# Cosine attention and GELU feed-forward on one core: swapped row sums added by tensor_reduce, values at piece ends, a first batch in a new order

## The chip, the core and the metric

The kernel runs on one core of a Trainium2 chip. TensorE (PE) multiplies matrices, VectorE (DVE), ScalarE (ACT) and GpSimd (POOL) work on rows of up to 128 partitions, and SyncE (SP) issues most of the transfers. Each engine takes its instructions in the order in which they stand in the program and waits for the others by semaphores. The metric is device time in microseconds (us), median of several runs.

## The reference

```python
q_n = q / (norm(q, axis=-1, keepdims=True) + 1e-06)          # q, k, v: (8, 12, 448, 64) float32
k_n = k / (norm(k, axis=-1, keepdims=True) + 1e-06)
scores = matmul(q_n, k_n.transpose(0, 1, 3, 2)) / tau        # tau = 0.1
attn = exp(scores - max(scores, axis=-1, keepdims=True))
attn = attn / (sum(attn, axis=-1, keepdims=True) + 1e-09)
x = matmul(attn, v).transpose(0, 2, 1, 3).reshape(8 * 448, 768)
h = x @ w_in                                                 # (768, 2048)
out = (0.5 * h * (1 + erf(h / sqrt(2)))) @ w_out             # (2048, 768); out is (3584, 768) float32
```

## The kernel before

The work goes batch by batch, and each batch of 12 heads goes in three groups of four heads (`g` counts the groups: `NQ = 3` a batch, 24 in all). A group passes these stations:

- `load_qk` brings q and k into a tile `qk` (four buffers, issued by SP). `square` squares them into `sq`, and `reduce` (DVE) adds the squares of each row into `nq`. `root` takes the square root as Ln and Exp on ACT (`lq`, `sr`), adds 1e-6 (`se`) and takes the reciprocal on DVE (`rn`). `scale` multiplies q and k by it into bf16 (`qkb`). From unit 3 on, squares and scales are POOL's. The list `units` cuts group 0 into two halves, so that unit numbers run one ahead of group numbers; `groups` says which units share one pass of `root`.
- `transposes` turns `qkb` into `qkT`: for the first batch on PE through PSUM with a copy by DVE, later by a transposing DMA on SP's queue.
- `scores` makes 7 passes a group: 4 matmuls into `st` and one exponential on ACT into `pt`. No maximum is subtracted, since the scores of unit vectors are bounded by 1/tau.
- `sums` multiplies by ones into the bank `sm`, where the row sums of a pair of heads stand in four stripes of 32 partitions, each sum as two halves in neighbouring stripes. `reciprocals` (DVE) transposes the bank (`tr`), swaps neighbouring stripes with four copies of 32 partitions x 28 numbers (`sw`), adds (`su`), takes reciprocals (`rc`) and spreads them by two transposes (`rs`). `values` multiplies `pt` by v into two PSUM banks (`o`), and `normalise` (DVE) multiplies these by `rs` into `x`. `both` is sums, reciprocals, values, normalise in this order.

Then `first(b)` computes `hp = x @ w_in` in 16 column tiles of 6 matmuls each and GELU on ACT. Its first 16 matmuls need only the first two groups of heads, the rest needs `x` of the third. The second product (`op`) of an earlier batch is cut into single matmuls, 16 to a *piece* (`second_pieces`), which `attention(b, fill)` strews between the passes: `plan` says how many of the 96 or 128 run ahead of each step `i`, and each step makes two passes (`group(b, i)`). Steps 5, 8 and 11 have `both`.

Pieces, `hp` tiles, PE transposes and the second bank of `values` take turns in two PSUM banks (`mm_tile`): with `aside=0` the values take the bank that the next piece wants, with `aside=1` the bank of the piece before, which a DVE copy (`ot`) empties. The first batch has no second product to strew; its order is written out in `attention_first`, with a few idle matmuls (`spin`). All orders are by hand; nothing reschedules them.

Of the kernel before, what the change touches and what calls it, by code (L numbers as in the profile page):

```python
# [8 lines left out]
F32 = mybir.dt.float32  # L9
# [6 lines left out]
def kernel(  # L16
# [81 lines left out]

    units = [(0, 0, 1), (0, 1, 2)] + [(g, 0, 2) for g in range(1, NG)]
    NU = len(units)  # L100
    groups = [[n] for n in range(NQ + 1)]
    for n in range(NQ + 1, NU, NQ):
        groups += [[n, n + 1], [n + 2]]
    place = {u: (n, j) for n, gr in enumerate(groups) for j, u in enumerate(gr)}
    qk_t, v_t, sq_t, nq_t, rn_t, qkb_t, qkT_t, pt_t = {}, {}, {}, {}, {}, {}, {}, {}
# [24 lines left out]
        for j in range(m):  # L130
            v_t[g + j] = t[:, j]

    def square(u):
        g, s0, s1 = units[u]
        if s0 == 0:
            sq_t[g] = sqp.tile([128, 2, 2, C, D], F32, tag="sq", name=f"sq{g}")
        sq, t = sq_t[g][:, :, s0:s1], qk_t[g][:, :, s0:s1]
        if u == 0:
            nc.scalar.activation(sq[:, 1], t[:, 1], AF.Square)
            nc.vector.tensor_tensor(sq[:, 0], t[:, 0], t[:, 0], ALU.mult)  # L140
        elif u == 1:
            nc.scalar.activation(sq, t, AF.Square)
        elif u == 2:
            nc.vector.tensor_tensor(sq[:, 0], t[:, 0], t[:, 0], ALU.mult)
            nc.gpsimd.tensor_tensor(sq[:, 1], t[:, 1], t[:, 1], ALU.mult)
        else:
            nc.gpsimd.tensor_tensor(sq, t, t, ALU.mult)  # L147

    def reduce(u):
# [41 lines left out]
    def transposes(u):  # L191
        g, s0, s1 = units[u]
        qkb = qkb_t[g]
        if s0 == 0:
# [7 lines left out]
        for i in range(2):  # L202
# [135 lines left out]

    def attention_first():
        x_t[0] = xp.tile([128, KD, S], BF16, tag="x", name="x0")  # L340
        scores(0, ((0, 0), (0, 1)))
        upto(root, 2)
        upto(scale, 2)
        upto(load_wi, 1)
        scores(0, ((0, 2), (0, 3)))
        upto(reduce, 3)
        upto(transposes, 2)
        scores(0, ((0, 4), (0, 5)))
        upto(root, 3)
        upto(square, 4)  # L350
        scores(0, ((1, 0), (1, 1)))
        upto(scale, 3)
        upto(reduce, 4)
        upto(load_v, 2)
        scores(0, ((1, 2), (1, 3)))
        upto(transposes, 3)
        upto(root, 4)
        scores(0, ((1, 4), (1, 5)))
        upto(scale, 4)
        upto(load_wi, 2)  # L360
        scores(0, ((0, 6), (1, 6)))
        spin(2)
        for c in range(C):
            if c == 2:
                sums(0)
                reciprocals(0)
            if c == 4:
                upto(transposes, 4)
            if c == 5:
                values(0)  # L370
                normalise(0)
            scores(1, ((0, c), (1, c)))
            if c == 0:
                upto(load_qk, 4)
            if c == 1:
                upto(load_wi, 3)
                upto(square, 5)
            if c == 3:
                upto(reduce, 5)
            if c == 4:  # L380
                upto(load_wi, 4)
        for c in range(C):
            if c == 2:
# [102 lines left out]
    upto(square, 1)  # L486
    upto(reduce, 1)
    upto(root, 1)
    upto(square, 2)
    upto(scale, 1)  # L490
    upto(transposes, 1)
    upto(reduce, 2)
    upto(square, 3)
    spin(2)
# [50 lines left out]
```

## Time and profile before

| | |
|---|---|
| median of 3 runs (lowest, highest) | 537.62 us (535.86, 537.73) |
| profiled execution, its own time | 534.5 us |
| its span, first to last instruction | 532.7 us |
| PE, DVE, ACT, POOL busy | 439.4, 243.7, 242.9, 171.5 us |
| mean granted clock of TensorE | 0.923 of full speed |

A busy share is an average over stages with different limits, so it does not say what an edit is worth; the stage in which the edit stands does. A granted clock of 1.00 is 2.4 GHz, 0.50 is 1.2 GHz.

### The profile page before, as it was taken

The numbers are of one execution on the slowest core, as the hardware profiler recorded it, in microseconds if no ns is written. First come the engines' busy times: TensorE is split into PE (matmuls) and PEld (weight loads), VectorE is DVE, ScalarE is ACT, GpSimd is POOL, SyncE is SP. The second block draws the span as 40 slices with busy tenths as digits, with TensorE's granted clock in tenths as the row PEclk, the third lists the DMA queues.
The fourth block names the chain that finished last, engine by engine and source line by source line (L and its number), as shares of the span: only waits on it lengthen the run. The fifth ranks groups of instructions, "written<-read, shape, count | busy, mean of one in ns | idle before, by whom it ended". The sixth has DMA issues, their size and how long they took to land.

```text
span 532.7 us, 8122 instructions
## 1 busy us (share of the span) xinstructions
PE 439.4 (82%) x3428; PEld 211.9 (40%) x3428; DVE 243.7 (46%) x387; ACT 242.9 (46%) x351; POOL 171.5 (32%) x113
## 2 busy tenths in 40 slices
PE   6626996859979599685997959777897959989996
PEld 3203442324435244242543425333353524434553
DVE  6596426582066801578026750557306591054011
ACT  4525465514655048341475326642365604762500
POOL 4871627070342505224061520807016070200000
PEclk9568999888999899797999989979799998999999
DMA  8896997172083902618037360635406440032013
GB/s 289 212 186 105 205 205 155 32 158 109 1 148 97 237 0 43 146 42 225 1 64 152 90 177 0 106 84 119 146 2 116 126 103 0 1 65 61 1 30 90
DMA packets 68340, 54.99 MB, mean 103 GB/s; under 512 B 40400, under 2 KB 63312, under 8 KB 68304
## 3 DMA queue, kind: packets, MB, share of 16 engines
q1 hardware_dynamic: 55888, 42.35, 31.2%
q0 software_dynamic: 12112, 11.80, 14.4%
q8 instruction: 27, 0.44, 0.4%
q10 hardware_dynamic: 304, 0.33, 0.2%
q14 instruction: 9, 0.07, 0.0%
HBM read 45.61 MB, written 11.01 MB: 106 GB/s over the span
## 4 chain that ended last, share of the span: by engine, by line
issue 44%; PE 23%; POOL 21%; DVE 8%; DMA 2%; ACT 1%; SPq 0%; POOLq 0%; DVEq 0%
PE hp L451 10%; POOL sq L147 10%; POOL qkb L187 9%; PE op L287 8%; DVE sw L253 4%; PE st L216 2%; PE o L241 1%; PE sm L230 1%; DMA qk<-in_k_dram 1%; ACT pt L220 1%; DVE rs L260 1%; POOL v L127 1%; DVE nq L157 1%; DVE x L266 1%; DVE tr L249 1%
## 5 line engine op out<-in xcount | busy, mean ns | idle before, releaser
L220 ACT ACTIVATE pt<-st 128x896 bf16<-128x896 f32 x168 | 145.2, 914 | 102.8 <-PE st L216 102.3
L451 PE MATMUL hp<-x,wi 128*128 128x448 bf16 x768 | 161.6, 373 | 34.1 <-DVE x L266 34.1
L287 PE MATMUL op<-wo,g 128*128 128x384 bf16 x896 | 162.8, 333 | 31.1 <-DVE x L266 31.1
L472 ACT ACTIVATE g<-hp 128x448 bf16<-128x448 f32 x128 | 67.6, 543 | 155.2 <-PE hp L451 155.1
L287 PEld LDWEIGHTS <-g 128*128 128x128 bf16 x896 | 83.5, 99 | 105.5 <-issue 57.4
L451 PEld LDWEIGHTS <-wi 128*128 128x128 bf16 x768 | 77.5, 102 | 117.5 <-issue 56.0
L174 POOL TENSOR_SCALAR se<-sr 128x56 f32<-128x56 f32 (+1 forms) x14 | 4.4, 312 | 266.4 <-ACT sr L173 266.4
L187 POOL TENSOR_TENSOR qkb<-qk,rn 128x896 bf16<-128x896 f32 (+1 forms) x48 | 79.1, 1674 | 13.8 <-DVE rn L176 13.8
L253 DVE COPY sw<-tr 32x28 f32<-32x28 f32 x96 | 72.3, 753 | 1.8
L176 DVE RECIPROCAL rn<-se 128x28 f32<-128x28 f32 (+2 forms) x18 | 6.9, 385 | 139.6 <-POOL se L174 139.4
L147 POOL TENSOR_TENSOR sq<-qk 128x1792 f32<-128x1792 f32 x22 | 69.9, 3178 | 0.2
L298 DVE COPY ot<-op 128x384 f32<-128x384 f32 x55 | 29.6, 539 | 70.7 <-PE op L287 70.7
L216 PE MATMUL st<-qkT 64*64 64x448 bf16 x672 | 56.8, 386 | 3.2 <-ACT pt L220 2.8
L157 DVE TENSOR_REDUCE nq<-sq 128x28 f32<-128x1792 f32 (+2 forms) x26 | 48.3, 1861 | 23.6 <-POOL sq L147 23.5
L241 PE MATMUL o<-pt,v 64*64 64x448 bf16 x672 | 38.4, 361 | 12.7 <-DVE qkT L206 12.1
L216 PEld LDWEIGHTS <-qkT 64*64 64x64 bf16 x672 | 17.5, 109 | 35.9 <-issue 30.5
L249 DVE STREAM_TRANSPOSE tr<-sm 128x448 f32<-128x448 f32 x24 | 15.5, 647 | 35.0 <-PE sm L230 35.0
L241 PEld LDWEIGHTS <-v 64*64 64x64 bf16 x672 | 18.8, 109 | 30.2 <-issue 21.4
L260 DVE STREAM_TRANSPOSE rs<-rc 128x448 f32<-128x448 f32 x48 | 28.1, 624 | 0.8
L266 DVE TENSOR_TENSOR x<-o,rs 128x448 bf16<-128x448 f32 x48 | 26.9, 597 | 2.4 <-PE o L241 2.4
L230 PE MATMUL sm<-pt,ones 128*32 128x448 bf16 x336 | 23.9, 371 | 0.4 <-ACT pt L220 0.4
L230 PEld LDWEIGHTS <-ones 128*32 128x32 bf16 x336 | 8.2, 98 | 13.0 <-issue 9.5
(38 smaller groups left out, 93.5 us busy)
## 6 DMA issues: line engine op xcount, KB each, us to landing
out_dram<-ot SPq DMA_DIRECT2D x54, 192.0 KB, 2.7
qk<-in_q_dram SPq DMA_DIRECT2D x23, 448.0 KB, 5.2
qk<-in_k_dram SPq DMA_DIRECT2D x23, 448.0 KB, 5.9
v<-in_v_dram POOLq DMA_DIRECT2D x7, 672.0 KB, 8.5
wi<-in_moe_w_in_dram POOLq DMA_DIRECT2D x8, 384.0 KB, 7.7
wo<-in_moe_w_out_dram POOLq DMA_DIRECT2D x4, 768.0 KB, 11.7
qk<-in_q_dram SPq DMA_DIRECT2D x2, 224.0 KB, 3.5
v<-in_v_dram POOLq DMA_DIRECT2D x1, 448.0 KB, 8.3
```

Of the source, the lines that this page charges most:

```text
L147: nc.gpsimd.tensor_tensor(sq, t, t, ALU.mult)
L157: nc.vector.tensor_reduce(nq[:, part], sq[:, part], mybir.AxisListType.X, ALU.add)
L187: eng.tensor_tensor(qkb[:, i, :, s0:s1].rearrange("p c s d -> p s c d"), t[:, i, s0:s1], rn[:, i].to_broadcast([128, s1 - s0, C, D]), ALU. ...
L216: nc.tensor.matmul(st[cols, n, :S], lhsT=qkT[rows, 1, c, cols], rhs=qkT[rows, 0, :, cols], start=True, stop=True, tile_position=(64 * s, 6 ...
L220: nc.scalar.activation(pt[:, :m], st[:, :m, :S], AF.Exp, scale=inv_tau)
L230: nc.tensor.matmul(bank_t[g, "sm"][r:r + 32, :S], lhsT=ones, rhs=pt_t[g, s, c], start=(c < 2), stop=(c >= C - 2), tile_position=(0, r))
L241: nc.tensor.matmul(bank_t[g, h][cols, :S], lhsT=v_t[g][rows, s, c, :], rhs=pt_t[g, s, c][rows], start=(c == 0), stop=(c == C - 1), tile_po ...
L253: nc.vector.tensor_copy(sw[32 * j:32 * (j + 1)], sums2[32 * (j ^ 1):32 * ((j ^ 1) + 1)])
L260: nc.vector.transpose(rs, rc[:, h].to_broadcast([128, NB, 32]))
L287: nc.tensor.matmul(ps[:, :NH], lhsT=g_t[sb][:, kf, t * 128:(t + 1) * 128], rhs=wo[:, kf, ni * NH:(ni + 1) * NH], start=(kf == 0), stop=(kf ...
L451: nc.tensor.matmul(hps[m], lhsT=wi[:, kd, m * 128:(m + 1) * 128], rhs=x_t[b][:, kd, :], start=(kd == 0), stop=(kd == KD - 1))
L472: nc.scalar.activation(g_t[sb][:, m, hf * S:(hf + 1) * S], hps.pop(m), AF.Gelu)
```

## The change

Five edits, in this order in the diff.

1. In `reciprocals` the four copies into `sw` become four `tensor_reduce` instructions that sum one number each, from the neighbouring stripe into column 1 of `tr` itself; the addition becomes a `tensor_reduce` over columns 0 and 1.
2. `plan` gives other numbers of fill matmuls, so that `both` in steps 5, 8 and 11 comes when a whole number of pieces has been issued. By the unchanged rule in its call, `aside` is then 1 at all three.
3. The `reduce` of step 4 moves to step 6, behind the first `both`.
4. The first batch is written in another order, `attention_first` now holding also what stood ahead of it; squares and scales of units 0 to 3 are split over ACT, DVE and POOL.
5. Units 5 and 6 (groups 4 and 5) share one `root`, and so `first(0)` scales and transposes group 3 alone; group 4 follows in step 1 of `attention(1)`.

```diff
-    groups = [[n] for n in range(NQ + 1)]
-    for n in range(NQ + 1, NU, NQ):
+    groups = [[n] for n in range(NQ + 2)] + [[NQ + 2, NQ + 3]]
+    for n in range(2 * NQ + 1, NU, NQ):
         groups += [[n, n + 1], [n + 2]]
...
-        for i, eng in enumerate((nc.vector if u <= 1 else nc.gpsimd, nc.gpsimd)):
+        for eng, i in parts or ((nc.gpsimd, 0), (nc.gpsimd, 1)):
...
-        sums2 = tr.rearrange("p b (k r) -> p k b r", k=2)[:, :, :, 0]
-        sw = rcp.tile([128, 2, NB], F32, tag="sw", name=f"sw{g}")
+        tr4 = tr.rearrange("p b (k r) -> p k b r", k=2)
         for j in range(4):
-            nc.vector.tensor_copy(sw[32 * j:32 * (j + 1)], sums2[32 * (j ^ 1):32 * ((j ^ 1) + 1)])
+            o = j ^ 1
+            nc.vector.tensor_reduce(tr4[32 * j:32 * (j + 1), :, :, 1], tr4[32 * o:32 * (o + 1), :, :, 0:1],
+                                    mybir.AxisListType.X, ALU.add)
         su = rcp.tile([128, 2, NB], F32, tag="su", name=f"su{g}")
-        nc.vector.tensor_tensor(su, sums2, sw, ALU.add)
+        nc.vector.tensor_reduce(su, tr4[:, :, :, 0:2], mybir.AxisListType.X, ALU.add)
...
     def attention_first():
+        square(2, ((AC, Q),))
+        scale(1, ((DV, 0), (GP, 1)))
+        square(3, ((GP, Q),))
+        scale(2, ((DV, 0), (GP, 1)))
...
+                scale(3, ((DV, 0), (GP, 1)))
                 sums(0)
...
-        plan = {96: (0, 18, 8, 8, 8, 0, 8, 8, 0, 8, 8, 22),
-                128: (0, 22, 12, 12, 12, 0, 12, 12, 0, 12, 12, 22)}[len(fill)]
+        plan = {96: (0, 18, 10, 10, 10, 0, 8, 8, 0, 8, 8, 16),
+                128: (0, 22, 14, 14, 14, 0, 16, 16, 0, 8, 8, 16)}[len(fill)]
...
             if i == 1:
-                upto(scale, nu)
-                upto(transposes, nu)
+                for n in (nu - 1, nu):
+                    upto(scale, n)
+                    upto(transposes, n)
...
-            if i in (4, 9):
-                upto(reduce, nu + (1 if i == 4 else 2))
+            if i in (6, 9):
+                upto(reduce, nu + (1 if i == 6 else 2))
...
-        for n in (nu + 1, nu + 2):
+        for n in (nu + 1, nu + 2) if b else (nu + 1,):
             upto(scale, n)
             upto(transposes, n)
```

Where the instructions stand, at three places. First, DVE in batch 1 (the second batch) at the first `both`; before:

```order
L298 COPY ot_1_869<-op_1_0_868 128x384
L157 TENSOR_REDUCE nq_964<-sq_913 128x28
L249 STREAM_TRANSPOSE tr_981<-sm_966 128x448
L253 COPY sw_983<-tr_981 32x28 x4
L255 TENSOR_TENSOR su_988<-tr_981,sw_983 128x28
```

and of the change:

```order
L295 COPY ot_2_922<-op_2_0_921 128x384
L243 STREAM_TRANSPOSE tr_988<-sm_973 128x448
L249 TENSOR_REDUCE tr_988<-tr_988 32x2x14 x4
L252 TENSOR_REDUCE su_994<-tr_988 128x28
L254 RECIPROCAL rc_996<-su_994 128x28
L257 STREAM_TRANSPOSE rs_0_998<-rc_996 128x448
L257 STREAM_TRANSPOSE rs_1_1000<-rc_996 128x448
L263 TENSOR_TENSOR x_842<-o_0_1002,rs_0_998 128x448
L263 TENSOR_TENSOR x_842<-o_1_1003,rs_1_1000 128x448
L151 TENSOR_REDUCE nq_1073<-sq_914 128x28
```

The sum of the norms' squares (`nq`) stood ahead of the transpose of the row sums and now stands behind `x`; one more piece is copied out (`ot`) ahead of it.

Second, POOL from `first(0)` into batch 1, where `sq_713` and `qkb_872` (before), `sq_706` and `qkb_871` (changed) are group 5; before:

```order
L187 TENSOR_TENSOR qkb_697<-qk_347,rn_674 128x2x7x64 x2
L187 TENSOR_TENSOR qkb_702<-qk_488,rn_674 128x2x7x64 x2
L147 TENSOR_TENSOR sq_713<-qk_491 128x1792
L174 TENSOR_SCALAR se_842<-sr_843 128x28
L187 TENSOR_TENSOR qkb_872<-qk_491,rn_846 128x2x7x64 x2
```

and of the change:

```order
L181 TENSOR_TENSOR qkb_698<-qk_336,rn_675 128x2x7x64 x2
L142 TENSOR_TENSOR sq_706<-qk_497 128x1792
L168 TENSOR_SCALAR se_836<-sr_837 128x56
L181 TENSOR_TENSOR qkb_866<-qk_390,rn_840 128x2x7x64 x2
L181 TENSOR_TENSOR qkb_871<-qk_497,rn_840 128x2x7x64 x2
```

The scaling of group 4 (`qkb_702` before, `qkb_866` now) has moved behind `se`, which waits for ACT in batch 1.

Third, DVE in the first batch from the norms of group 2 (`qk_133`) to the row sums of group 0 (`sm_361`, `sm_364`); before:

```order
L170 TENSOR_REDUCE se_313<-root_1_119 128x28
L176 RECIPROCAL rn_316<-se_313 128x28
L249 STREAM_TRANSPOSE tr_376<-sm_361 128x448
L253 COPY sw_378<-tr_376 32x28 x4
L255 TENSOR_TENSOR su_383<-tr_376,sw_378 128x28
```

and of the change:

```order
L164 TENSOR_REDUCE se_356<-root_1_119 128x28
L170 RECIPROCAL rn_359<-se_356 128x28
L181 TENSOR_TENSOR qkb_361<-qk_133,rn_359 128x2x7x64
L200 COPY qkT_407<-tp_0_408 128x896
L200 COPY qkT_407<-tp_1_417 128x896
L243 STREAM_TRANSPOSE tr_426<-sm_364 128x448
L249 TENSOR_REDUCE tr_426<-tr_426 32x2x14 x4
```

DVE now scales the q of group 2 itself, and its two copies of that group's transposes have moved from behind the row sums of group 0 to ahead of them.

## Rows read from the trace of the kernel before

**Rows 1.** Stretches: start:end, length, busy us per engine, PEclk, DMA share, GB/s.

```profile
0.00:55.70 55.70, 32.19 (x295) 14.71 (x295) 38.21 (x61) 24.44 (x35) 32.50 (x33) 0.75 0.90 198
55.70:74.05 18.35, 18.35 (x99) 9.30 (x96) 5.58 (x9) 7.82 (x15) 10.18 (x6) 1.00 1.32 189
74.05:111.32 37.27, 30.72 (x307) 14.30 (x307) 18.31 (x34) 22.07 (x28) 14.45 (x10) 0.95 0.47 120
111.32:489.05 377.73, 319.03 (x2512) 151.80 (x2509) 174.54 (x271) 179.88 (x256) 114.42 (x67) 0.93 0.39 90
```

**Rows 2.** Stretches as in rows 1: one 128-fill attention, one `hp`, the last attention.

```profile
137.17:173.97 36.80, 33.95 (x340) 16.69 (x339) 19.44 (x36) 22.19 (x28) 14.39 (x9) 1.00 0.42 92
429.61:456.76 27.15, 21.46 (x100) 10.01 (x96) 11.15 (x11) 7.93 (x15) 6.49 (x4) 0.87 0.22 45
456.76:489.05 32.29, 29.34 (x307) 14.01 (x307) 12.79 (x34) 21.59 (x26) 3.61 (x3) 1.00 0.19 43
```

**Rows 3.** Who waited for whom: us in total, times, longest us.

```profile
PE hp L451 <- DVE x L266: 34.1, 6, 5.7
PE op L287 <- DVE x L266: 31.1, 11, 5.1
```

**Rows 4.** Groups of instructions by shape: count, busy us, mean ns of one.

```profile
L253 DVE COPY sw<-tr 32x28 f32<-32x28 f32 x96 | 72.3, 753 | 1.8
L187 POOL TENSOR_TENSOR qkb<-qk,rn 128x448 bf16<-128x448 f32 x2 | 2.7, 1370 | 2.2 <-DVE rn L176 2.2
L170 DVE TENSOR_REDUCE se<-root 128x28 f32<-128x56 f32 x2 | 0.4, 206 | 0.5 <-ACT root L169 0.5
```

**Rows 5.** Timeline (start us, us, instruction, [idle before]) around batch 2's third row sums.

```profile
170.69 6.63 POOL L187 TENSOR_TENSOR qkb<-qk,rn 128x896 bf16<-128x896 f32 x4 [0.62 <-DVE rn L176]
173.31 7.18 DVE L253 COPY sw<-tr 32x28 f32<-32x28 f32 x4
177.28 3.17 POOL L147 TENSOR_TENSOR sq<-qk 128x1792 f32<-128x1792 f32 x1
182.86 18.16 PE L451 MATMUL hp<-x,wi 128*128 128x448 bf16 x80 [5.69 <-DVE x L266]
```

**Rows 6.** Timeline around the first row sums of batch 1.

```profile
85.51 2.02 DVE L157 TENSOR_REDUCE nq<-sq 128x28 f32<-128x1792 f32 x1 [3.59 <-POOL sq L147]
88.12 2.02 DVE L253 COPY sw<-tr 32x28 f32<-32x28 f32 x4
93.04 0.80 PE L287 MATMUL op<-wo,g 128*128 128x384 bf16 x2 [5.09 <-DVE x L266]
```

**Rows 7.** Timeline of the last batch's third row sums, and the closing `op` matmuls.

```profile
487.71 0.65 DVE L249 STREAM_TRANSPOSE tr<-sm 128x448 f32<-128x448 f32 x1 [0.31 <-PE sm L230]
490.87 1.12 DVE L266 TENSOR_TENSOR x<-o,rs 128x448 bf16<-128x448 f32 x2
...
507.22 20.96 PE L287 MATMUL op<-wo,g 128*128 128x384 bf16 x128
```

**Rows 8.** Timeline of the first batch.

```profile
15.01 3.18 POOL L147 TENSOR_TENSOR sq<-qk 128x1792 f32<-128x1792 f32 x1
16.61 0.21 DVE L170 TENSOR_REDUCE se<-root 128x28 f32<-128x56 f32 x1 [0.54 <-ACT root L169]
22.50 0.62 DVE L206 COPY qkT<-tp 128x896 bf16<-128x896 bf16 x1 [1.02 <-PE tp L205]
23.39 3.49 ACT L220 ACTIVATE pt<-st 128x896 bf16<-128x896 f32 x4 [2.53 <-PE st L216]
28.09 9.30 DVE L253 COPY sw<-tr 32x28 f32<-32x28 f32 x4
41.69 2.82 PE L241 MATMUL o<-pt,v 64*64 64x448 bf16 x27 [12.06 <-DVE qkT L206]
```

**Rows 9.** Timeline of batch 1's first scale.

```profile
79.01 3.34 POOL L187 TENSOR_TENSOR qkb<-qk,rn 128x896 bf16<-128x896 f32 x2 [0.45 <-DVE rn L176]
```

**Rows 10.** DMA issues: count, median us from issue to landing.

```profile
qkT<-qkb SPq DMA_TRANSPOSE x21, 4.1
```

More of the change, by code (lines that the diff above doesn't have):

```diff
@@ L131, in load_v, with square, reduce @@
             v_t[g + j] = t[:, j]
-    def square(u):
+    def square(u, parts=None):
         g, s0, s1 = units[u]
-        if s0 == 0:
+        if g not in sq_t:
             sq_t[g] = sqp.tile([128, 2, 2, C, D], F32, tag="sq", name=f"sq{g}")
         sq, t = sq_t[g][:, :, s0:s1], qk_t[g][:, :, s0:s1]
[L138 to L149, printed above, removed]
+        for eng, part in parts or ((nc.gpsimd, slice(0, 2)),):
+            if eng is nc.scalar:
+                eng.activation(sq[:, part], t[:, part], AF.Square)
+            else:
+                eng.tensor_tensor(sq[:, part], t[:, part], t[:, part], ALU.mult)
+    def reduce(u, part=slice(0, 2)):
         g, s0, s1 = units[u]
@@ L152, in reduce @@
         n, j = place[u]
-        if j == 0:
+        if n not in nq_t:
             nq_t[n] = nrm.tile([128, len(groups[n]), 2, s1 - s0, C], F32, tag="nq", name=f"nq{n}")
         nq = nq_t[n][:, j]
-        for part in ((slice(0, 1), slice(1, 2)) if u == 0 else (slice(0, 2),)):
-            nc.vector.tensor_reduce(nq[:, part], sq[:, part], mybir.AxisListType.X, ALU.add)
+        nc.vector.tensor_reduce(nq[:, part], sq[:, part], mybir.AxisListType.X, ALU.add)
     def root(n):
@@ L177, in root, with scale @@
         rn_t[n] = rn
-    def scale(u):
+    def scale(u, parts=None):
         g, s0, s1 = units[u]
@@ L189, in scale, with transposes @@
                 rn[:, i].to_broadcast([128, s1 - s0, C, D]), ALU.mult)
-    def transposes(u):
+    def transposes(u, parts=(0, 1)):
         g, s0, s1 = units[u]
         qkb = qkb_t[g]
-        if s0 == 0:
+        if g not in qkT_t:
             qkT_t[g] = qkTp.tile([128, 2, C, 128], BF16, tag="qkT", name=f"qkT{g}")
@@ L201, in transposes @@
         rows = slice(64 * s0, 64 * s1)
-        for i in range(2):
+        for i in parts:
             tp = mm_tile(f"tp{u}_{i}", (128, C, 128), BF16)
@@ L340, in attention_first @@
         x_t[0] = xp.tile([128, KD, S], BF16, tag="x", name="x0")
+        DV, AC, GP = nc.vector, nc.scalar, nc.gpsimd
+        Q, K, QK = slice(0, 1), slice(1, 2), slice(0, 2)
+        square(0, ((AC, K), (DV, Q)))
+        reduce(0, Q)
+        reduce(0, K)
+        upto(root, 1)
+        square(1, ((AC, QK),))
+        scale(0, ((DV, 0), (GP, 1)))
+        upto(load_wi, 1)
+        reduce(1)
+        transposes(0)
+        square(2, ((AC, Q),))
+        upto(root, 2)
+        square(2, ((AC, K),))
@@ L341, in attention_first @@
+        spin(2)
         scores(0, ((0, 0), (0, 1)))
-        upto(root, 2)
-        upto(scale, 2)
-        upto(load_wi, 1)
         scores(0, ((0, 2), (0, 3)))
-        upto(reduce, 3)
-        upto(transposes, 2)
+        scale(1, ((DV, 0), (GP, 1)))
+        reduce(2, Q)
+        transposes(1, (0,))
         scores(0, ((0, 4), (0, 5)))
-        upto(root, 3)
[L350 to L353, printed above, removed]
-        upto(load_v, 2)
@@ L355, in attention_first @@
[L355 to L362, printed above, removed]
+        transposes(1, (1,))
+        square(3, ((GP, Q),))
+        reduce(2, K)
+        upto(load_wi, 2)
+        scores(0, ((1, 0), (1, 1)))
+        reduce(3, Q)
+        upto(root, 3)
+        scale(2, ((DV, 0), (GP, 1)))
+        square(3, ((GP, K),))
+        scores(0, ((1, 2), (1, 3)))
@@ L363, in attention_first @@
+        spin(2)
+        scores(0, ((1, 4), (1, 5)))
+        transposes(2, (0,))
+        spin(1)
+        transposes(2, (1,))
+        scores(0, ((0, 6), (1, 6)))
+        upto(load_v, 2)
+        upto(load_wi, 3)
+        upto(load_qk, 4)
         for c in range(C):
             if c == 2:
+                reduce(3, K)
+                upto(root, 4)
+                scale(3, ((DV, 0), (GP, 1)))
                 sums(0)
+            if c == 5:
+                transposes(3)
                 reciprocals(0)
-            if c == 4:
-                upto(transposes, 4)
@@ L369, in attention_first @@
-            if c == 5:
+            scores(1, ((0, c), (1, c)))
+            if c == 2:
+                done[square] = done[reduce] = done[scale] = done[transposes] = 4
+                upto(square, 5)
+                upto(load_wi, 4)
+                upto(load_qk, 5)
+            if c == 6:
                 values(0)
                 normalise(0)
[L372 to L377, printed above, removed]
@@ L378, in attention_first @@
-            if c == 3:
[L379 to L383, printed above, removed]
+        for c in range(C):
+            if c == 3:
                 sums(1)
                 reciprocals(1)
-            if c == 4:
+            if c == 5:
                 values(1)
@@ L390, in attention_first @@
             if c == 0:
+                upto(square, 6)
+                upto(load_wo, 2)
                 upto(load_qk, 6)
-                upto(square, 6)
-            if c == 3:
-                upto(reduce, 6)
+            if c == 4:
+                upto(reduce, 5)
                 upto(load_v, 3)
-        upto(load_wo, 2)
         sums(2)
@@ L459, in first @@
         upto(load_wo, 4)
-        for n in (nu + 1, nu + 2):
+        for n in (nu + 1, nu + 2) if b else (nu + 1,):
             upto(scale, n)
             upto(transposes, n)
-        upto(load_qk, (b + 1) * NQ + 5)
+        upto(load_qk, (b + 1) * NQ + (5 if b else 4))
         upto(square, nu + 3)
@@ L485 @@
     upto(load_v, 1)
[L486 to L494, printed above, removed]
     fill = []
```

4 lines of the change are left out of this document (3 added, 1 removed).

## Prediction

> **What bounds the kernel now.** I read the stretches first, cut where a batch passes from `hp` to attention [rows 1, 2]. In a stretch without disturbance PE has hardly a gap: the first `hp` is 18.35 us long and 18.35 us busy at a granted clock of 1.00 [rows 1]. The reader is to see how this differs from the sixth `hp`, the same 96 matmuls: 27.15 us, with 21.46 busy at 0.87 [rows 2]. So PE sets the length, and what can be won is its gaps and the slow matmuls that follow a gap.
>
> The waits say whom PE waits for: `x` of DVE, 34.1 us ahead of `hp` and 31.1 us ahead of `op` [rows 3]. In the timeline DVE is late because of the copies into `sw`. They move 28 numbers, and the four of one batch took 7.18 us, from 173.31 to 180.49. In that time POOL works without a break: four scales from 170.69 on (1.66 us each), then a square that ends at 180.45 [rows 5]. The last copy ends when POOL does. The other copies bear this out by their mean, 753 ns for 28 numbers [rows 4]. PE then stands 5.69 us ahead of `hp` [rows 5].
>
> At the first `both` of a batch there is a second cause: `nq` (2.02 us, itself waiting for POOL's square) stands ahead of the row sums' transpose, the copies take 2.02, and PE stands 5.09 us [rows 6]. In the first batch the copies take 9.30 us, and behind them wait the two `qkT` copies of the next group: PE stands 12.06 us [rows 8].
>
> **The change, part by part.**
>
> *The reductions.* The trace has no reduction that reads another stripe than it writes. The nearest is L170, 56 numbers into 28 on DVE: 206 ns [rows 4], and one of these ran at 16.61, in the middle of a POOL square (15.01 to 18.19), in 0.21 us [rows 8]. A copy from the neighbouring stripe in the same circumstances would have stood until 18.19. I therefore take about 0.2 us for each new reduction, whatever POOL does. The chain is then what the last batch shows, where POOL was idle: from the transpose at 487.71 to the end of `x` at 491.99, 4.28 us [rows 7]. The bounds are 4.28, and the 4.28 + 6.4 of a batch whose copies wait (7.18 less some 0.75 unhindered).
>
> *What 4.28 us meets.* Ahead of `hp` PE has the values and 16 matmuls of 18.35 / 96 = 0.19 us, 3.06 us, before it needs the third `x`. In the last batch that covered the chain: `hp` begins there at 489.05 [rows 1] and needs `x` at 492.1; the first half of `x` is done at 491.5. So I take every `hp` as 18.35. The slack is 0.6 us, and the cover would be gone with a chain of 4.9.
>
> *`nq` behind the row sums.* The 2.02 us no longer delay `tr`. They come behind `x`, where the next PE piece does not wait for them.
>
> *Values at piece ends.* Now the values take the bank of the next piece, so that after 6 `op` matmuls PE must wait for `x`; this leaves gaps even in the last batch, where nothing else is wrong: 32.29 long, 29.34 busy [rows 2]. At a piece end with the other bank, 16 matmuls of 20.96 / 128 = 0.16 us [rows 7] plus two passes of scores stand ahead of that wait, over 3.5 us behind the values, which covers the chain. The values themselves wait for the `ot` copy of the finished piece; the sums run meanwhile. So I take the attention stretches as their busy part at clock 1.00: 29.34 with 96 fill matmuls, 33.95 with 128 [rows 2].
>
> *Group 4 in batch 1.* This edit costs. Now scaling in batch 1 starts at 79.01 [rows 9], 4.96 us after the stretch begins, and serves the third group only. Changed, it must serve the second: 3.34 us of scales, then the transposing DMA, 4.1 us to landing [rows 10], which gives 12.4 us, and some 0.4 more since root and reciprocal now take two groups. Its first scores stand behind seven passes and 18 + 10 + 10 matmuls: 38 x 0.16 = 6.2, with the passes (four matmuls each, about 0.07 each since they run side by side) 8.2 us. PE waits 4.5 us, and its clock then falls as after the 5.09 us gap: that stretch has 30.72 busy against 29.34 at full clock, 1.4 us [rows 1, 2]. The stretch of batch 1 becomes 29.34 + 4.5 + 1.4 = 35.2.
>
> *The first batch.* Removing the stall alone gives 55.70 - 8.6 = 47.1. The order gives more. The K side of group 1 has POOL to itself: with the reciprocals no later than now, DVE copies its transposes at 20.6 to 21.6, against 23.12 (22.50 + 0.62) [rows 8]. Then 15 exponentials follow, one left of group 0 and 7 each of groups 1 and 2, at 3.49 / 4 = 0.87 us [rows 8]: 13.1 us. Between them stands one root (0.5). ACT also runs dry twice, since PE does the values of group 0 ahead of the first scores of group 2, and those of group 1 ahead of its last two: each takes 2.82 us at half clock [rows 8] and half of that at full clock, of which the second is partly covered, so 2.7 to 5 us. The last exponential ends at 37 to 40; the last sums and values add 2.4 (1.4 for the values at full clock, and two thirds of that for half as many, less overlapped sums). `hp` starts at 39.4 to 42.6, and I take 42, near the end at which the clock stays as low as now (0.75) [rows 1].
>
> One row speaks against the split. A POOL scale of 448 columns took 1370 ns [rows 4] where one of 896 took 1.66 us [rows 5]: both of the short ones ran beside DVE's half of the same scale. Half of 1.66 is 0.83, so up to 0.5 us were lost beside it, and a split of twice the columns may lose twice that, 1.1 us, on the path through K. Group 1 and group 2 each have such a split; K of group 2 has some slack behind Q's transposes, so I take 0.7 in all, within the 39.4 to 42.6. The Trainium skill (SBUF — State Buffer, section "Who interferes with whom") says that a Vector instruction with two SBUF inputs contends with a GpSimd instruction that reads SBUF, and that whoever issues first decides who blocks. By that rule POOL would lose the whole of DVE's half each time and the sum would be up to 1.5 us longer, without it 0.7 shorter; the 1370 ns agree with it in sign.
>
> *The sum*, against the profiled span: 42.0 + 7 x 18.35 + 35.2 + 3 x 33.95 + 3 x 29.34 + 43.65 (the end, 532.70 - 489.05, unchanged) = 439.2. Seven `hp` stretches, batches 2, 4, 6 with 128, batches 3, 5, 7 with 96. The part 111.32 to 489.05, 377.73 now, becomes 6 x 18.35 + 101.85 + 88.02 = 300. With the 1.8 us outside the span (534.5 - 532.7) it is 441. The median shown is 0.6% above its profiled execution (537.62 / 534.5), so 444 us.
>
> **The rivals.**
>
> *The opening is bound by transfers.* The DMA share is 0.90 over 55.70 us [rows 1], 50 us of transfers. If `hp` needs nearly all of them first, it starts near 50, and the time is 452. Against it: the share holds loads for batch 1 and part of `w_out`, and `hp` wants the second half of `w_in` only 9 us after it starts.
>
> *The reductions wait for POOL as the copies do.* Then the change does not do what it says. For it: no row shows a reduction across stripes. The `hp` stretches stay as they are, about 8 us too long in each of six, the opening keeps some 6 us of stall. The moved `nq` and the bank still save their part. 439 + 48 + 6 = 493, with the rest 497. Against it: L170's 0.21 us beside the square.
>
> *Slower: the small reductions are slow in themselves,* through the stripe shift or through column 1 being written into the tile that is read. There are five in each of 24 chains; the covers leave about 0.7 us a chain. To eat 96 us, a chain must grow by 4.7, each reduction by 0.95 us. From 1.15 us each on, the kernel is slower, at 2 us each about 545 to 560. For it: the reductions of 1792 numbers take 2.02 [rows 6]. Against it: those read 64 times as much, and at 28 numbers the rows show 0.2.
>
> **How the numbers follow.** The forecast, 444, has 0.76, with its own range 434 to 456: the low end if the wait in batch 1 is hidden (-6) and the opening takes 39 (-3), the high end if each of 14 stretches keeps 0.5 us of gap (+7) and the opening keeps 47 (+5). The transfers' rival has 0.11, the waiting reductions 0.07, slow reductions 0.025, other mixtures 0.035. The range 433 to 464 holds the first two and more. Half a per cent, 2.7 us, is about what a measurement of this kernel can tell from no change; both likely cases lie far beyond. Faster 0.955, the same 0.015, slower 0.03.
>
> **What would show it.** The reductions in `reciprocals`: 0.17 to 0.25 us each and no long ones. PE's wait for `x` ahead of `hp` gone from the list of waits, all `hp` stretches 18.3 to 18.6 at clock 1.00. Attention stretches of about 29.5 and 34. In batch 1 a PE wait of 4 to 5 us for `qkT`, from the transposing DMA. The first `hp` at 40 to 43. I am wrong if a reduction ends with a POOL instruction, if another wait (`ot` for the values, ACT's exponentials ahead of the sums now that only 16 matmuls stand there instead of 22) opens in each batch, or if the first `hp` waits for `w_in`.

## The result, and the profile after

| | before | after |
|---|---|---|
| median (lowest, highest), 4 runs each | 536.74 us (534.62, 537.73) | 439.66 us (437.64, 441.08) |
| ratio of the medians, 95% interval | | 0.8193 [0.8149, 0.8237] |
| profiled execution, its span | 534.5, 532.7 us | 441.08, 439.3 us |
| PE, DVE, ACT, POOL busy | 439.4, 243.7, 242.9, 171.5 us | 420.7, 193.4, 244.1, 168.4 us |
| mean granted clock | 0.923 | 0.974 |

The kernel takes 18% less time. The forecast was 444, its sum of spans 439.2; the span of the profiled execution is 439.3, and that execution is the longest of the four (435.8 to 439.3). Of all executions behind the figures below one is left out: it took 927.79 us, with the old opening, where the four others took 441.09 to 442.42.

The stretches of the kernel after, in the columns of rows 1: up to the first `hp`, the first `hp`, batch 1, an `hp`, an attention with 128 fill matmuls, one with 96, and the end.

```profile
0.00:41.94 41.94, 32.92 (x296) 15.55 (x296) 29.69 (x65) 25.95 (x37) 29.71 (x31) 0.82 1.05 245
41.94:61.75 19.81, 19.44 (x98) 9.63 (x97) 6.34 (x7) 8.16 (x16) 6.47 (x3) 0.94 1.30 186
61.75:96.42 34.67, 30.88 (x307) 14.57 (x307) 17.40 (x37) 22.01 (x28) 16.82 (x11) 0.95 0.63 145
96.42:114.69 18.27, 18.27 (x103) 9.31 (x100) 4.94 (x8) 7.83 (x15) 7.39 (x4) 1.00 0.65 167
114.69:148.59 33.90, 33.90 (x340) 16.79 (x339) 18.54 (x39) 22.19 (x28) 13.43 (x9) 1.00 0.45 100
166.85:195.98 29.13, 29.13 (x308) 14.31 (x307) 17.24 (x37) 22.08 (x28) 13.42 (x9) 1.00 0.47 104
394.77:439.30 44.53, 39.13 (x228) 21.83 (x224) 7.17 (x15) 8.69 (x17) 0.00 (x0) 0.97 0.17 42
```

From 96.42 to 394.77 PE has no gap and a clock of 1.00: length and busy time agree in each row, where [rows 2] had 27.15 against 21.46. What gaps are left lie in the first 97 us and behind PE's last matmul.

The costliest waits of PE after, as in rows 3.

```profile
PE st L210 <- DMA qkT<-qkb: 4.2, 2, 3.8
PE st L210 <- ACT pt L214: 1.7, 3, 0.8
PE tp L199 <- DVE qkb L181: 1.6, 1, 1.6
PE o L235 <- DVE x L263: 1.6, 2, 1.4
```

The 34.1 us ahead of `hp` and 31.1 us ahead of `op` [rows 3] are gone. New is the wait for a transposing DMA, 3.8 us in one piece, the one that the forecast set at 4.5.

The groups by shape after, as in rows 4.

```profile
L249 DVE TENSOR_REDUCE tr<-tr 32x28 f32<-32x28 f32 x96 | 18.8, 196 | 1.8
L252 DVE TENSOR_REDUCE su<-tr 128x28 f32<-128x56 f32 x24 | 5.1, 211 | 0.8
L181 DVE TENSOR_TENSOR qkb<-qk,rn 128x896 bf16<-128x896 f32 x2 | 2.2, 1091 | 0.1
```

The 96 swaps take 196 ns each instead of 753 [rows 4]. The timeline after shows them beside a working POOL, and three other places:

```profile
16.50 1.09 DVE L181 TENSOR_TENSOR qkb<-qk,rn 128x896 bf16<-128x896 f32 x1
16.55 2.58 POOL L181 TENSOR_TENSOR qkb<-qk,rn 128x896 bf16<-128x896 f32 x1 [1.41 <-DVE rn L170]
47.85 5.17 SPq L192 DMA_TRANSPOSE qkT<-qkb  x1
69.92 4.82 SPq L192 DMA_TRANSPOSE qkT<-qkb  x2
73.93 0.38 PE L210 MATMUL st<-qkT 64*64 64x448 bf16 x4 [3.79 <-DMA qkT<-qkb]
94.06 6.62 POOL L181 TENSOR_TENSOR qkb<-qk,rn 128x896 bf16<-128x896 f32 x4 [0.62 <-DVE rn L170]
95.76 0.83 DVE L249 TENSOR_REDUCE tr<-tr 32x28 f32<-32x28 f32 x4
```

At 95.76 four reductions take 0.83 us in all while POOL scales from 94.06 to 100.68; in [rows 5] four copies took 7.18 in such a place. At 16.50 it is POOL that is slow: its half of a split scale takes 2.58 us beside DVE's 1.09, where a scale without such company takes 1.66 [rows 5].

The transposing DMAs after, in the columns of rows 10: the one issued at 47.85, and all.

```profile
qkT<-qkb SPq DMA_TRANSPOSE x1, 13.9
...
qkT<-qkb SPq DMA_TRANSPOSE x21, 4.0
```

The one at 47.85, group 3's, lands at about 61.7: 13.9 us at a DMA share of 1.30, against 4.0 in the median. The first scores of batch 1 begin at 61.75. So the end of the first `hp` stretch is set by this transfer; more of that below.

### The profile page after: what moved, and what is told of

It reads as the page before. It is cut to its first block, busy times and chain, and to the rows that moved or that the text cites. A ratio compares the mean times of both kernels' runs of the same rounds, so it can differ in the third digit from the quotient of the medians.

```text
span 439.3 us, 8129 instructions
## 1 busy us (share of the span) xinstructions
PE 420.7 (96%) x3429; PEld 210.5 (48%) x3429; DVE 193.4 (44%) x390; ACT 244.1 (56%) x353; POOL 168.4 (38%) x111
## 4 chain that ended last, share of the span: by engine, by line
PE 90%; POOL 2%; DVE 2%; issue 2%; DMA 1%; ACT 1%; POOLq 0%
PE hp L468 34%; PE op L284 33%; PE st L210 9%; PE o L235 8%; PE sm L224 4%; PE spin L334 2%; POOL qkb L181 2%; DMA qkT<-qkb 1%; ACT pt L214 1%; PE tp L199 1%; DVE nq L151 1%; DMA out_dram<-ot 0%; DVE qkT L200 0%; POOL sq L142 0%; ACT L491 0%
## 5 line engine op out<-in xcount | busy, mean ns | idle before, releaser
L284 PE MATMUL op<-wo,g 128*128 128x384 bf16 x896 | 157.7, 328 | 0.0
L468 PE MATMUL hp<-x,wi 128*128 128x448 bf16 x768 | 147.8, 354 | 0.0
L468 PEld LDWEIGHTS <-wi 128*128 128x128 bf16 x768 | 74.8, 98 | 72.7 <-issue 4.5
L181 POOL TENSOR_TENSOR qkb<-qk,rn 128x896 bf16<-128x896 f32 (+1 forms) x46 | 77.6, 1713 | 14.6 <-DVE rn L170 14.6
L168 POOL TENSOR_SCALAR se<-sr 128x28 f32<-128x28 f32 (+1 forms) x14 | 4.4, 312 | 180.2 <-ACT sr L167 180.2
L142 POOL TENSOR_TENSOR sq<-qk 128x1792 f32<-128x1792 f32 (+1 forms) x23 | 70.0, 3044 | 6.3 <-DMA qk<-in_k_dram 6.2
L210 PE MATMUL st<-qkT 64*64 64x448 bf16 x672 | 54.4, 373 | 7.0 <-DMA qkT<-qkb 4.2
L170 DVE RECIPROCAL rn<-se 128x28 f32<-128x28 f32 (+2 forms) x18 | 6.9, 385 | 99.1 <-POOL se L168 98.9
L249 DVE TENSOR_REDUCE tr<-tr 32x28 f32<-32x28 f32 x96 | 18.8, 196 | 1.8
L224 PEld LDWEIGHTS <-ones 128*32 128x32 bf16 x336 | 8.2, 97 | 13.3 <-issue 9.6
```

What stands on the lines that cost most here:

```text
L142: eng.tensor_tensor(sq[:, part], t[:, part], t[:, part], ALU.mult)
L181: eng.tensor_tensor(qkb[:, i, :, s0:s1].rearrange("p c s d -> p s c d"), t[:, i, s0:s1], rn[:, i].to_broadcast([128, s1 - s0, C, D]), ALU. ...
L210: nc.tensor.matmul(st[cols, n, :S], lhsT=qkT[rows, 1, c, cols], rhs=qkT[rows, 0, :, cols], start=True, stop=True, tile_position=(64 * s, 6 ...
L224: nc.tensor.matmul(bank_t[g, "sm"][r:r + 32, :S], lhsT=ones, rhs=pt_t[g, s, c], start=(c < 2), stop=(c >= C - 2), tile_position=(0, r))
L284: nc.tensor.matmul(ps[:, :NH], lhsT=g_t[sb][:, kf, t * 128:(t + 1) * 128], rhs=wo[:, kf, ni * NH:(ni + 1) * NH], start=(kf == 0), stop=(kf ...
L468: nc.tensor.matmul(hps[m], lhsT=wi[:, kd, m * 128:(m + 1) * 128], rhs=x_t[b][:, kd, :], start=(kd == 0), stop=(kd == KD - 1))
```

## The experiments

The kernel before is run beside each; ratios are to it. Edits carry the numbers of the list in "The change".

**Edit 1 alone.** The kernel before with `reciprocals` of the change (the hunk of L249 to L252) and nothing else.

> The kernel before with the first edit alone (the halves swapped and added by tensor_reduce). Theory, the copies wait for POOL and reductions do not: the reductions take 0.17 to 0.25 us each, the wait ahead of hp goes, so six hp stretches fall from 26.5 to 18.4 us (-48); in the opening the stall of 12 us falls to about 5.5, since the next norms' sum still waits for POOL's square there (-6.4 and some clock); in attention the wait of 5.1 falls to about 3.9 in three batches and 2.85 to 1.6 in three (-8). Time 469 to 474. Rival, the reductions wait for POOL as the copies do: 535 to 540. Rival, the order and the piece ends are what counts: over 500.

Measured: 473.12 us (472.36 to 475.13), 0.8821 [0.8791, 0.885]. All `hp` stretches are now 18.26 to 18.27, where the six after the first had 25.65 to 27.15; one of them:

```profile
106.64:124.91 18.27, 18.27 (x102) 9.31 (x99) 4.94 (x8) 7.83 (x15) 6.42 (x4) 1.00 0.68 169
```

What it does not reach is the wait ahead of `op`, here in the list of waits:

```profile
PE op L288 <- DVE x L267: 24.4, 11, 3.9
```

So edit 1 carries 63 of the 97 us when it goes in alone (68 when it is taken out of the change, next), and the wait for `x` inside the attentions has another cause than the copies.

**The changed kernel with the copies back.** All else as changed.

```diff
...
-            nc.vector.tensor_reduce(tr4[32 * j:32 * (j + 1), :, :, 1], tr4[32 * o:32 * (o + 1), :, :, 0:1], ...)
+            nc.vector.tensor_copy(sw[32 * j:32 * (j + 1)], sums2[32 * (j ^ 1):32 * ((j ^ 1) + 1)])
...
-        nc.vector.tensor_reduce(su, tr4[:, :, :, 0:2], mybir.AxisListType.X, ALU.add)
+        nc.vector.tensor_tensor(su, sums2, sw, ALU.add)
```

> The changed kernel with the four copies and the two-input addition put back, all else as changed. Theory: the copies take about 7.2 us at every third row sum again, hp grows by some 8 us in six batches (+48), the opening by 1 to 3; in attention the piece ends cover the rest. Time 487 to 493. Rival, the new order and the piece ends carry most of the gain: below 465.

Measured: 507.69 us (505.86 to 513.13), 0.9487 [0.9428, 0.9546]. The direction was right, the size 15 us short. Its timeline shows why (the first three rows are in batch 1):

```profile
83.44 3.17 POOL L142 TENSOR_TENSOR sq<-qk 128x1792 f32<-128x1792 f32 x1 [4.13 <-DMA qk<-in_k_dram]
83.60 3.05 DVE L251 TENSOR_TENSOR su<-tr,sw 128x28 f32<-128x28 f32 x1
91.70 2.75 PE L235 MATMUL o<-pt,v 64*64 64x448 bf16 x27 [2.57 <-DVE ot L294]
101.45 6.63 POOL L181 TENSOR_TENSOR qkb<-qk,rn 128x896 bf16<-128x896 f32 x4 [0.62 <-DVE rn L170]
103.16 8.09 DVE L249 COPY sw<-tr 32x28 f32<-32x28 f32 x4
108.03 3.17 POOL L142 TENSOR_TENSOR sq<-qk 128x1792 f32<-128x1792 f32 x1
113.61 11.64 PE L467 MATMUL hp<-x,wi 128*128 128x448 bf16 x46 [6.60 <-DVE x L262]
```

The copies of 103.16 end at 111.25, with POOL's square of 108.03 (to 111.20): PE stands 6.60 us, and such an `hp` is 27.6 to 27.8 long (6 x 9.4 = 57 us in all). Two things were not expected. The addition of two tiles waits like a copy: 3.05 us at 83.60, to the end of the square. And the attentions with 96 fill matmuls are 33.5 instead of 29.1: behind a late chain on DVE the copy `ot` comes late, and the values at a piece end wait for it (2.57 us at 91.70, three such waits in all).

**Only the four swaps as copies**, in place, the sum kept a reduction.

```diff
-            nc.vector.tensor_reduce(tr4[32 * j:32 * (j + 1), :, :, 1], tr4[32 * o:32 * (o + 1), :, :, 0:1], ...)
+            nc.vector.tensor_copy(tr4[32 * j:32 * (j + 1), :, :, 1], tr4[32 * o:32 * (o + 1), :, :, 0])
```

> The changed kernel with the four swaps as tensor_copy into the same column of tr, the addition still a tensor_reduce; so only the kind of the four instructions differs from the changed kernel. Theory, a copy from SBUF to SBUF waits for POOL's running instruction and a reduction does not: the four take some 5 us at the third row sums of six batches, hp grows by 3 to 6 us there, the attentions with 96 fill matmuls by 2 to 4, the opening by 3; 475 to 492. Rival, the other tile and the two-input addition made the old form wait: 439 to 442.

Measured: 489.68 us (488.79 to 494.41), 0.9138 [0.9099, 0.9178]. The group in its trace:

```profile
L249 DVE COPY tr<-tr 32x28 f32<-32x28 f32 x96 | 58.9, 614 | 1.8
```

The same bytes from and to the same places take 614 ns as a copy and 196 as a reduction, so the operation decides.

**Only the sum as an addition of two inputs.**

```diff
-        nc.vector.tensor_reduce(su, tr4[:, :, :, 0:2], mybir.AxisListType.X, ALU.add)
+        nc.vector.tensor_tensor(su, tr4[:, :, :, 0], tr4[:, :, :, 1], ALU.add)
```

> The changed kernel with the final addition as a tensor_tensor of two SBUF inputs instead of a tensor_reduce; the four swaps stay reductions. Theory of the shared read port: where POOL is scaling or squaring, the addition takes 0.2 us plus what is left of POOL's instruction, up to 1.7 or 3.2 us; at the third row sums the slack ahead of hp is 0.6 us, so 0 to 1 us is lost in each of six batches: 440 to 446. Rival, only the copies share a port with POOL: the addition takes 0.20 us everywhere, 439 to 441.

Measured: 447.03 us (446.7 to 448.4), 0.8343 [0.8322, 0.8365]; 1 us above the range. In its timeline, beside a square, and beside a scale ahead of an `hp`:

```profile
179.44 3.19 POOL L142 TENSOR_TENSOR sq<-qk 128x1792 f32<-128x1792 f32 x1
180.35 2.35 DVE L252 TENSOR_TENSOR su<-tr 128x28 f32<-128x28 f32 x1
...
197.61 6.63 POOL L181 TENSOR_TENSOR qkb<-qk,rn 128x896 bf16<-128x896 f32 x4 [0.62 <-DVE rn L170]
200.11 0.90 DVE L252 TENSOR_TENSOR su<-tr 128x28 f32<-128x28 f32 x1
203.67 0.54 PE L468 MATMUL hp<-x,wi 128*128 128x448 bf16 x2 [0.18 <-DVE x L263]
```

The first addition ends with the square, at 182.7. The second takes 0.90 instead of 0.21: the chain from the transpose (198.57) to the end of `x` (203.62) is 5.05 us, and PE stands 0.18 us ahead of `hp`. So the cover ends at 4.87; the prediction had put it at a chain of 4.9. Each of the six `hp` is only 0.5 to 0.6 us longer. Most of the loss is in two attentions with 96 fill matmuls, 32.8 and 31.3 us instead of 29.1: there the late chain delays `ot`, and the values wait for it (4.1 us in two waits), which the expectation had left out.

**The copies into PSUM.** The swaps stay copies and the sum an addition, but the copies go to free columns of the bank `sm`.

```diff
...
+        sw = sm[:, S:S + 2 * NB].rearrange("p (k b) -> p k b", k=2)
...
+            nc.vector.tensor_copy(sw[32 * j:32 * (j + 1)], tr4[32 * o:32 * (o + 1), :, :, 0])
...
+        nc.vector.tensor_tensor(su, tr4[:, :, :, 0], sw, ALU.add)
```

> The changed kernel with the four swaps as tensor_copy from SBUF into the unused columns of the PSUM bank of the row sums, and the addition as a tensor_tensor of one SBUF and one PSUM input. Theory, what waits for POOL is an instruction that needs a second SBUF port of DVE: these need none, so 0.17 to 0.3 us a copy and 0.2 to 0.3 for the addition, everywhere; 439 to 442. Rival, a copy as such waits: as with copies in place, 475 or more.

Measured: 440.63 us (439.45 to 441.37), 0.8205 [0.8187, 0.8222], as fast as the change. Its groups:

```profile
L251 DVE COPY sm<-tr 32x28 f32<-32x28 f32 x96 | 19.7, 205 | 3.3
L253 DVE TENSOR_TENSOR su<-tr,sm 128x28 f32<-128x28 f32 x24 | 4.8, 200 | 0.8
```

None of the 96 copies takes more than 0.22 us, and none of the 24 additions more than 0.21. So a copy from SBUF into PSUM did not wait for POOL, nor did an addition with one input there. Together the change and the last three kernels say what the wait hangs on: a copy from SBUF to SBUF and an addition of two SBUF inputs wait, a reduction does not, and neither do the copy and the addition with an operand in PSUM. The Trainium skill (SBUF — State Buffer, section "Who interferes with whom") says the same of the forms in SBUF: VectorE shares its second pair of ports with GpSimd, a copy or a second SBUF input can take it, a reduction never does. The trace agrees, with 614 and 587 ns (means of the copy and of the addition) against 196 to 211.

**The old fill numbers** (edit 2 undone).

```diff
-        plan = {96: (0, 18, 10, 10, 10, 0, 8, 8, 0, 8, 8, 16),
-                128: (0, 22, 14, 14, 14, 0, 16, 16, 0, 8, 8, 16)}[len(fill)]
+        plan = {96: (0, 18, 8, 8, 8, 0, 8, 8, 0, 8, 8, 22),
+                128: (0, 22, 12, 12, 12, 0, 12, 12, 0, 12, 12, 22)}[len(fill)]
```

> The changed kernel with the old numbers of fill matmuls, so that the values no longer come at piece ends and take the bank of the next piece. Theory: PE waits 1.46 us for x twice in each of the four attentions with 96 fill matmuls and once in each of the three with 128: +16, time 454 to 458. Rival, PE would wait for ACT's exponentials there anyway: +5 or less, up to 445.

Measured: 458.46 us (456.87 to 458.98), 0.8547 [0.8519, 0.8575]; 0.5 us above the range. The attentions have 35.5 and 32.5 us instead of 33.9 and 29.1. One of eleven such gaps in its timeline:

```profile
133.83 1.14 PE L284 MATMUL op<-wo,g 128*128 128x384 bf16 x6 [1.55 <-DVE x L263]
```

No swap is slow here; the 17.2 us of wait come from the place and the bank of the values alone. Values at piece ends are worth 19 us by the medians (15.8 by the spans of the two profiled executions).

**The norms' sums back ahead of the row sums** (edit 3 undone: `if i in (4, 9)`).

> The changed kernel with the norms' sum of step 4 back ahead of the first row sums. Theory: the chain of the row sums grows by up to 2.4 us to 6.7, against a cover of some 5.2, in the attentions with 96 fill matmuls (three, the last has no norms to sum), nothing in those with 128, where POOL's square is done earlier: +3 to +6, 442 to 446. Rival, the piece ends cover it all: no change, 439 to 441.

Measured: 438.92 us (438.22 to 439.56), 0.8187 [0.8163, 0.8211]. The theory missed, the rival held: the attentions become 34.4 (+0.5) and 28.9 (-0.2). With a piece between values and wait, 2 us more on DVE are covered but for one wait of 0.4 us in each of the three attentions with 128, where the theory had expected nothing. Under the old fill numbers the edit would count: edit 1 alone, with the sums ahead, has 35.6 and 37.1 in its attentions of batches 2 to 6, the kernel with the old fill numbers, with the sums behind, 35.5 and 32.5.

**The old opening.** The kernel before with edits 1 to 3.

> The kernel before with edits 1, 2 and 3 (reductions, piece ends, norms' sum behind the row sums), but its own opening and its own root groups. Theory: the first hp starts at 47 to 50 us instead of 41.9, batch 1 has no wait for the transposing DMA (29.5 us instead of 34.7), all else as changed: 439 to 443, so that the new opening and the late group 4 about cancel. Rival, the new opening is worth what it saves in itself: 445 or more.

Measured: 441.76 us (441.09 to 442.42), 0.824 [0.822, 0.8261]; the span of its profiled execution is 439.4, like that of the change. Its stretches:

```profile
0.00:50.05 50.05, 34.77 (x295) 16.40 (x295) 29.82 (x62) 24.55 (x35) 32.44 (x33) 0.76 1.00 221
50.05:68.31 18.26, 18.26 (x99) 9.30 (x97) 5.12 (x8) 7.83 (x15) 10.18 (x6) 1.00 1.30 193
68.31:97.44 29.13, 29.13 (x308) 14.25 (x307) 17.24 (x37) 22.08 (x28) 13.48 (x9) 1.00 0.63 152
```

Beside the rows of after: the new opening is 8.1 us shorter, the first `hp` 1.5 longer and batch 1 5.5 longer. Edits 4 and 5 nearly cancel: by the medians they win 2 to 3 us together.

**Group 4 early again** (edit 5 undone in the changed kernel).

```diff
-    groups = [[n] for n in range(NQ + 2)] + [[NQ + 2, NQ + 3]]
-    for n in range(2 * NQ + 1, NU, NQ):
+    groups = [[n] for n in range(NQ + 1)]
+    for n in range(NQ + 1, NU, NQ):
...
+        upto(reduce, 6)
...
-        for n in (nu + 1, nu + 2) if b else (nu + 1,):
+        for n in (nu + 1, nu + 2):
...
-        upto(load_qk, (b + 1) * NQ + (5 if b else 4))
+        upto(load_qk, (b + 1) * NQ + 5)
```

> The changed kernel with group 4 rooted, scaled and transposed together with group 3 in the first feed-forward again (the fifth edit undone; its norms' sum stands behind the third x of the opening). Theory: PE's wait of 3.8 us for the transposing DMA in batch 1 goes, and some 1.4 us of slow clock behind it; GELU starts about 1 us later without delaying PE. Time 434 to 436. Rival, the transposing DMAs of groups 3 and 4 then land too late for the first scores of batch 1, among the loads of w_out: PE waits there instead, 439 to 442.

Measured: 435.11 us (433.82 to 439.03, 6 runs), 0.8128 [0.8098, 0.8157]: the best of all. Its stretches:

```profile
41.23:61.56 20.33, 19.21 (x98) 9.49 (x96) 6.28 (x7) 10.19 (x20) 11.94 (x8) 0.96 1.26 181
61.56:90.66 29.10, 29.10 (x306) 14.15 (x307) 17.23 (x37) 21.50 (x27) 13.48 (x9) 1.00 0.74 175
```

Batch 1 goes from 34.67 to 29.10, with no gap. The changed kernel run once more gave 439.01 (438.58 to 440.33), 0.8181 [0.8163, 0.8198]:

> The changed kernel once more, on the same chip as the others of this call, to compare with the version with group 4 early: 437.6 to 441.1, and a wait for the transposing DMA in batch 1 that differs from 3.8 us (2 to 4.5), since other kernels with the same opening showed 1.8 to 4.2.

Its wait in batch 1 is 3.1 us. So edit 5 costs about 4 us; the interval just misses that of this second measurement of the change, and overlaps that of the first.

**The opening's split scales whole on POOL.**

```diff
-        scale(2, ((DV, 0), (GP, 1)))
+        scale(2)
...
-                scale(3, ((DV, 0), (GP, 1)))
+                scale(3)
```

> The changed kernel with both halves of the opening's two 896-column scales on POOL. Now DVE's half takes 1.09 and POOL's half beside it 2.58 us. Theory: on POOL alone they take 1.67 each, so k is ready 0.75 us later and q 0.6 later, twice: the first hp starts 0.7 to 1.7 us later (now 41.9). Time 440 to 442. Rival, the split costs as much through the shared port as it saves: no change of that start within 0.4 us.

Measured: 440.58 us (439.87 to 441.9), 0.8219 [0.8198, 0.8239]. POOL's part of its timeline, and its first `hp` stretch:

```profile
16.47 3.33 POOL L181 TENSOR_TENSOR qkb<-qk,rn 128x896 bf16<-128x896 f32 x2 [1.41 <-DVE rn L170]
```

```profile
43.34:63.13 19.79, 18.33 (x99) 9.30 (x96) 6.82 (x9) 9.24 (x17) 6.76 (x4) 1.00 1.32 185
```

Alone, POOL needs 1.67 for a scale, so beside DVE's half it lost 0.92 of that half's 1.09. The split still wins 1.4 us of opening (41.94 against 43.34; three other runs with the opening of the change begin `hp` at 41.1 to 41.4). In the medians that is 0.9 to 1.6 us, within the intervals. The second row matters more: here the clock is 1.00 and PE busy 18.33, and the stretch is as long as in the change, since group 3's transfer lands late.

**A steady clock into the first `hp`.** The kernel with group 4 early, and 18 idle matmuls more in the opening: `spin(2, 0)` behind each of the seven score passes of its third loop, `spin(4, 0)` behind its last row sums.

> The kernel with group 4 early, and two idle matmuls behind each of the seven last score passes of the opening and four behind its last row sums, in the bank that is free there. Theory, the first hp takes 20.3 instead of 18.3 us because PE had little to do in the ten us before: with the idle matmuls the clock stays at 2.4 GHz, the first hp takes 18.3 to 18.8 us and begins no later than 41.5: 432 to 434. Rival, the idle matmuls delay the scores and the first hp begins 1 us or more later: 435 or more.

Measured: 442.52 us (440.13 to 442.61), 0.8227 [0.8206, 0.8248]; the theory missed, the rival held. The idle matmuls waited for a bank that values still held, in the list of waits:

```profile
PE spin L334 <- DVE x L263: 4.9, 2, 3.0
```

The first `hp` began at 49.73, not 41.2. This kernel could not test what it was made for; the landing of group 3's transfer answers it otherwise, below.

## Why the prediction was right, step by step

**The reductions** were put at 0.2 us whatever POOL does, from L170 beside a square. Measured 0.196 and 0.211, none long; the rival that they wait like copies had been priced at 493. The kernel with copies shows that branch: 489.7 with copies alone, 507.7 with the addition too. The price had left two things out, the addition's own wait and the values' wait for `ot`. The price of the third rival does not come out: by its own terms, five reductions of 2 us grow a chain by some 9 us, 8.3 beyond the cover, and 24 chains make about 640 us, not 545 to 560. Nothing in the forecast uses it.

**The cover ahead of `hp`**, 16 matmuls and the values with 0.6 us to spare: six stretches of 18.26 to 18.27 (said 18.35), and the addition experiment shows the edge at 4.87, where 4.9 was said.

**Values at piece ends**: 33.9 and 29.1 (said 33.95 and 29.34). The cover, "over 3.5 us", is 3.2 by the prediction's own prices for 16 matmuls and two passes; in the trace four passes stand there, and with 128 fill matmuls it is 3.7. **`nq` behind the row sums** was named as a removal of 2.02 us without a term of its own; beside edit 2 it is worth about 1 us by the stretches (three times 0.5 less twice 0.2), too little to tell in the medians.

**Group 4 in batch 1** was priced at 4.5 + 1.4: the wait is 3.8, the busy time 30.88 against 29.13 without the gap (1.75), and the stretch 34.67 (said 35.2). This term is the least steady of the sum: in the experiments that keep edits 4 and 5, the wait for group 4's transfer shrinks as that for group 3's, at the end of the first `hp`, grows (below), and the two sum to 2.9 to 4.4 us.

**The first batch**: `hp` begins at 41.94 (said 42), but that the term is right to 0.06 is luck: two errors inside it offset. The last exponential ends at 37.62 (said 37 to 40), and from there to `hp` it takes 4.32 (said 2.4). PE waits for the `x` of the group before, which frees the bank of its values and stands behind an `nq` on DVE, and the last values then take 2.39 us instead of 1.4, at a clock of 0.87 between 37.6 and 41.94:

```profile
36.87 1.98 DVE L151 TENSOR_REDUCE nq<-sq 128x28 f32<-128x1792 f32 x1
38.76 1.14 DVE L263 TENSOR_TENSOR x<-o,rs 128x448 bf16<-128x448 f32 x2
39.43 0.35 PE L235 MATMUL o<-pt,v 64*64 64x448 bf16 x1 [1.40 <-DVE x L263]
```

Nor does removing the stall alone give 47.1: with the reductions and the old opening `hp` begins at 51.37 (edit 1) and 50.05 (edits 1 to 3). The split was taken at 0.7 for both together; POOL lost 0.92 at each, K of group 2 having slack. By the rule of the Trainium skill named in the prediction (SBUF — State Buffer, section "Who interferes with whom") POOL would lose the whole of DVE's half; the row gives 0.92 of 1.09, near to the rule, and near to the 1.1 that the prediction had scaled up from the short scales.

**Two mis-sized terms.** The first of the "7 x 18.35" measured 19.81. In the change's own trace that looks like clock, 19.44 busy at 0.94, with a wait of 0.4. But the stretch with the scales whole on POOL has 18.33 busy at 1.00 and is 19.79 long, with a wait of 1.5. In both the end is the landing of group 3's transposing DMA: 47.85 + 13.9 = 61.75 and 49.78 + 13.3 = 63.1; with group 4 early 51.36 + 10.2 = 61.56. So the rival "bound by transfers" is there in small: not ahead of `hp`, but at its end, where a transposing DMA of usually 4 us takes 10 to 16, at the highest DMA share of the stretches. Of the 8.1 us that the opening won, 1.5 were given back. In ten runs with the new opening this transfer is issued between 46.4 and 52.0 us, and it lands between 61.5 and 63.7 whenever it was issued: with the old fill numbers `hp` begins 0.9 us earlier than in the change, at 41.08, and batch 1 not before 62.13. Loads of `w_out` are in flight beside it, the last from 40.82 to 61.2 in the change; whether they hold it up is not shown, since no run changes these loads alone. That a steadier clock would win nothing there follows from these landings, not from a run of its own. The other term is the end, 44.53 for 43.65; PE has finished its part after 39.13 us in both, and in the second run of the change the end is 43.6 (437.6 - 394.01), so the 0.9 are scatter of the last transfer.

The errors (+1.46, +0.88, -0.53 in batch 1, -1.62 in the other stretches and -0.06 in the opening) sum to 0.1. That the sum meets the span so closely is luck, then: the mechanisms held, the two mis-sized terms were offset by small errors the other way, and the execution compared is the longest of four. **The scaling** from 441 to 444 then moved the forecast away: it took the profiled execution to lie 0.6% below the median, as before, while after it is the highest of four.

Where the 97 us came from, in medians:

| | us |
|---|---|
| before | 536.1 to 536.9 |
| edit 1 | 473.1 |
| edits 1 to 3 | 441.8 |
| all five | 439.0 to 439.7 |
| all but edit 5 | 435.1 |

## What to carry to other kernels

Look in the timeline for small VectorE instructions that end when a GpSimd instruction ends; if they copy SBUF to SBUF or read two SBUF inputs, a reduction over one element or an operand in PSUM does the same work in 0.2 us. Price such a stall by all that stands behind it in the queue: here a copy of 28 numbers delayed `x`, and with it `hp`, and by way of `ot` the values too. And where an opening gets shorter, ask which transfers then meet: a wait can hide in a stretch whose engine looks merely slow, and another kernel with a different clock there tells the two apart.

## What the runs showed of the hardware that was not expected

- What began second waited. A two-input addition of 28 numbers that comes second waits for POOL (2.35 and 3.05 us); where DVE's two-input scale began 0.05 us ahead of POOL's, POOL waited (2.58 instead of 1.66 us).
- A copy into PSUM is free of this (205 ns mean, none over 0.22 us), though it reads SBUF as the others do.
- A transposing DMA of 4.0 us in the median took, for group 3 in the first `hp`, 10.0 to 15.6 us to landing in the ten runs with the new opening, where it was issued early, and 7.3 to 9.4 in the three kernels with the old one; the DMA share of that stretch is 1.25 to 1.32.
